# A retention layer and a Mish layer on one core: the first tiles' keys for the states turned back by TensorE, the decay moved into the keys, and three steps moved

## The chip, the core and the metric

The kernel runs on one core of one Trainium2 chip. The metric is the device time of one execution in microseconds. Fewer is better. The profile beside it is of one execution, recorded by the hardware profiler.

## What is computed

Attention without a softmax, with a decay that depends on the distance (retention), for 8 batches, 8 heads, 576 positions and heads of 64; its output, with the heads side by side, is x with 4608 rows of 512, and goes through two products (512 to 2048 and back) with a Mish between.

```python
scores = scale * np.matmul(q, k.transpose(0, 1, 3, 2))
gamma = 1.0 - 2.0 ** (-5.0 - np.arange(H, dtype=np.float32))
Dmat = np.where(rel >= 0, gamma[:, None, None] ** rel[None, :, :], 0.0)   # rel = pos[:, None] - pos[None, :]
ret = scores * Dmat[None, :, :, :]
attn = np.matmul(ret, v)                      # x: attn as (B * S, H * D)
h = x @ w_in
g = h * np.tanh(np.log1p(np.exp(h)))          # Mish
out = g @ w_out
```

## The kernel before

**Chunks and tiles.** The 576 positions of a batch are cut into chunks of 128 (and one of 64, two batches of which share a chunk). There are 36 chunks. Four chunks make a tile of 512 rows, so there are nine tiles; chunks 0 to 7 are the first 128 positions of the eight batches and make tiles 0 and 1. A chunk's output is the product of its own scores (masked) with v, and of q with a state, the sum of kᵀv over all positions ahead of it, with the decay multiplied into k or v. For each tile `g1` (L553) makes 16 blocks of Mish(x w_in), four products of 128x512 each, and `g2` (L569) or `g2_first` (L590) the product with w_out, 16 for each row block. These 128x512 products all go through `product` (L525), which can split one into two halves of 256 columns: `halved[0]` says how many of the next ones.

**The first two tiles** have a way of their own. `load_first_qk` (L102) loads q and k of four batches, cast to bf16 on the way; q of batches 0 and 1 comes as float32 by two loads of SyncE (L121) and is cast by VectorE (L639). `f_transpose` (L185) turns q and k, so that the head dimension lies on the partitions, `f_scores` (L208) makes the scores and multiplies them by the decay, `f_v` (L228) casts v, and `f_out` (L236) multiplies and copies the result to x of its tile (`xts`). In tile 0 each batch is copied by itself (L253), in tile 1 two batches at a time (L255). `keep_warm` (L167) issues products of zeros that nobody reads, which fill TensorE's waits at the start.

**The states of the first chunk.** When chunk 1 of a batch is handled, `states` (L383) also needs kᵀv of the batch's chunk 0. For that, `load_k0` (L263) loads k of the first 128 positions a second time, not turned, by GpSimd's queue, `cast_k0` (L267) casts it to bf16, and `f_state` (L257) multiplies v by the decay (`gv`). Loads, casts and products are spread over the whole kernel: a load each at L681, L712, L742, L785 and four at L815; casts at L729, L731 and by the table `cast_at` (L778).

**The other chunks** go two at a time through `visit` (L498), in this order on TensorE: part of the next pair's state products, this pair's outputs, the next pair's scores, the rest. `outputs_copy` (L485) then copies the two banks to `xts`, one by ScalarE and one by VectorE (L490), and `step_m` (L351) multiplies the next pair's scores by the mask. Ahead of that, each chunk needs `load` (q, k and v by GpSimd's queue), `step_p` (VectorE scales q and k, two instructions, L304), `step_v` (decay into v; GpSimd from chunk 20 on, L311) and `step_t` (turns q and k: by TensorE up to chunk 15, by a DMA transpose of SyncE from chunk 16 on, L333). `hold` (L492) makes GpSimd wait for such a transpose, and the loads behind it with it. `more_loads` can tie a load to a product of TensorE (`newest`), and `step_t` a transpose.

**The order is written out by hand.** Every engine takes its instructions in the order of the program. Tiles 0 and 1 are written as a list of calls and the table `steps` (L695): steps of tile 1 between the blocks of tile 0's second product. Then come 24 units (L726), and then a loop over the tiles from 2 on (L776) in which n is the pair of chunks visited and w a step of eight; the visit is at w = 6. There, of the chunks n+4 and n+5, one is scaled at w = 4 and the other at w = 7 (transpose behind each) as long as n+4 is at most `NPE` = 18; later both are scaled at w = 4 and 5 and turned at w = 6.

PSUM: scores, transposes and tile 1's outputs share the slots "sc" (two, of two banks each), blocks of `g1` the slots "hp" (two), row blocks "ops" (one), and the states "st" (one).

Of the kernel before, what the change touches and what calls it, by code (L numbers as in the profile page):

```python
# [16 lines left out]
def kernel(  # L17
# [100 lines left out]
        nc.gpsimd.dma_start(out=pair, in_=v[ds(b, 2), :, 0:P, :].rearrange("b h p d -> p (b h) d"))  # L118

    for b in range(2):  # L120
        nc.sync.dma_start(out=q0[:, b, :], in_=q[b, :, 0:P, :].rearrange("h (g r) d -> g h (r d)", r=8))  # L121
    for b in range(2):
        load_first_qk(0, 1, b)

# [103 lines left out]
    def f_v(t, b, copy):  # L228
        vb = first.tile([P, H, D], BF16, name="vb", bufs=4)
        copies = copy if isinstance(copy, tuple) else (copy,)  # L230
        n = H // len(copies)
        for j, copy in enumerate(copies):
            copy(vb[:, ds(n * j, n), :], v0[4 * t + b][:, ds(n * j, n), :])
        fst[t]["vb"][b] = vb

    def f_out(t, b, copy):  # L236
        if b == 0:
            xts[t] = xp.tile([P, KC, NCH * P], BF16, name="xT")
        vb = fst[t]["vb"][b]
        if t == 0:  # L240
            pool, name = ((ps_h, "hp"), (ps_h, "hp"), (ps_st, "st"), (ps_o, "ops"))[b]
            ot = pool.tile([P, NP, P], F32, name=name)
        else:
            if b % 2 == 0:
                fst[1]["out"] = ps_sc.tile([P, 2, NP, P], F32, name="sc")
            ot = fst[1]["out"][:, b % 2]
        for p in range(NP):
            for e in range(2):
                nc.tensor.matmul(ot[ds(64 * e, 64), p, :], lhsT=vb[:, 2 * p + e, :],
                                 rhs=fst[t]["sm", b][:, 2 * p + e, :],  # L250
                                 start=(p == 0), stop=True, skip_group_check=True)
        if t == 0:
            copy(xts[t][:, :, ts(b, P)], ot)  # L253
        elif b % 2:
            copy(xts[1].rearrange("p h (b i) -> p b h i", i=P)[:, ds(b - 1, 2)], fst[1]["out"])  # L255

    def f_state(t, b, engine=nc.gpsimd):  # L257

        n = 4 * t + b
        v0s[n] = first.tile([P, H, D], BF16, name="v0s", bufs=B)  # L260
        engine.tensor_tensor(v0s[n], v0[n], gv[:, 0, :].unsqueeze(2).to_broadcast([P, H, D]), op=OP.mult)

    def load_k0(b):  # L263
        k0r[b] = first.tile([P, H, D], F32, name="k0r", bufs=2)
        nc.gpsimd.dma_start(out=k0r[b], in_=k[b, :, 0:P, :].rearrange("h p d -> p h d"))

    def cast_k0(b, copy=nc.scalar.copy):  # L267
        k0[b] = first.tile([P, H, D], BF16, name="k0", bufs=3)
        copy(k0[b], k0r[b])

# [380 lines left out]
    keep_warm(1)  # L653
    f_out(0, 0, act)
    f_out(0, 1, act)
    keep_warm(5, ps_st, "st")
    load_w_in(1536, 512)
    f_v(0, 3, (dve, dve))
    f_v(0, 2, (act, pool))
# [17 lines left out]
                                base=0, pattern=[[1, 64]], channel_multiplier=-1)  # L677
    for b in range(4):
        load(N0 + b)
        if b == 0:  # L680
            load_k0(0)  # L681
    nc.vector.tensor_scalar(gq, gq, 1.0 / math.sqrt(D), None, op0=OP.mult)
    for b in range(4):
        f_state(0, b, nc.vector)


    for f in range(2):
        g1(0, f, 2, begun[f])
    g1_pair(2)
    for f in range(4, nF):  # L690
        halved[0] = 2 if f > 6 else 1
        g1(0, f)
    for i in range(2):
        f_mix(0, i)
    steps = {0: "T0", 3: "S0 C1", 9: "T1", 11: "S1", 12: "V0 V1 V2 V3", 14: "O0 O1", 15: "O2 O3"}  # L695
    for i in range(nF):
        for step in steps.get(i, "").split():
            n = int(step[1])
            if step[0] == "T":
                for j in range(2):  # L700
                    f_transpose(1, n, j, [(ps_sc, "sc", (dve, act)[j])])
            elif step[0] == "S":
                f_scores(1, n)
            elif step[0] == "V":
                f_v(1, n, dve if n == 3 else act)
            elif step[0] == "C":
                for j in range(2):
                    f_mix(n, j)
            else:
                f_out(1, n, (dve, act)[n // 2])  # L710
        g2_first(i // 4, i % 4)
    load_k0(1)  # L712

    queued = [4 * NCH]

# [9 lines left out]
    ts_ = {3: 0, 7: 1, 12: 2, 14: 3, 19: 4, 21: 5}  # L725
    for u in range(24):  # L726
        j, w = divmod(u, 4)
        if u == 5:
            cast_k0(0)  # L729
        elif u == 14:  # L730
            cast_k0(1, dve)  # L731
        halved[0] = 2 if 0 < u < 6 else 0
        if u in ps:
            att(N0 + ps[u], "P")
        if u == 11:
            step_m(N0)
        if u in vs:
            att(N0 + vs[u], "V")
        if w == 0 and j > 0:
            if j < 5:  # L740
                if j == 4:
                    load_k0(2)  # L742
                load(N0 + j + 3)
            else:
                load(N0 + j + 3)
                queued[0] += 1
        if u == 10:
            units, early = states(N0)
            seen = written(units[0]())
            step_s(N0)  # L750
            units[1]()
            units[2](seen)
            run(sums)
        elif u == 16:
            att(N0 + 4, "P")
        elif u == 17:
            visit(N0, ((ps_o, "ops"), (ps_h, "hp")), (act, act))
            run(sums)
        elif u == 22:
            visit(N0 + 2, ((ps_h, "hp"), (ps_h, "hp")), (act, dve))  # L760
        if u == 20:
            stores(act)
        if u in (13, 20):
            run(casts, dve if u == 13 else act)
        if u in ts_:
            att(N0 + ts_[u], "T")
        stores()
        if u < nF:
            g1(1, u, 2 if u == 0 else 1)
            flush()  # L770
        else:
            g2(1, u - nF)


    cast_at = {12: 2, 16: 3, 20: 4, 22: 5, 26: 6, 30: 7}
    for t in range(2, nT + 1):  # L776
        for i in range(nF):
            n, w = NCH * (t + 1) + i // 8 * 2, i % 8  # L778
            if w == 2 and n in cast_at:
                cast_k0(cast_at[n])  # L780
            if w == 2:
                run(casts, act)
                halved[0] = {14: 16, 20: 29}.get(n, 0)
            if w == 6 and n + 4 == NPE:
                load_k0(3)  # L785
            if w == 6 and n < n_chunks:
                visit(n, ((ps_h, "hp"), (ps_h, "hp")), (act, dve), lambda: g2(t - 1, i))
            if w == 0:
                stores(act if n == N0 + 4 else dve)
                run(sums)  # L790
            if w == 7 and n + 2 == NPE:
                stores()
            if w in (0, 1) and n + 2 < NT:
                att(n + 2 + w, "P")
            if w in ((3, 4) if n + 2 < NPE else (0, 1)):
                att(n + 2 + (w in (1, 4)), "V")
            if w in ((4, 7) if n + 4 <= NPE else (4, 5)) and n + 4 >= NT:
                stores()
                att(n + 4 + (w != 4), "P")
            if w == 7 and NT <= n + 4 <= NPE:  # L800
                step_t(n + 5, newest[0])
            if w == 5 and 16 <= n < 24:
                f_state(1, n // 2 - 8, nc.vector)


            if w in (1, 3) and n + 2 == NT:
                more_loads(n + 5 + w // 3, newest[0])
            if w == 1 and n + 2 == NPE:
                more_loads(n + 5, newest[0])
            if w == 1 and NPE < n + 2 < n_chunks:  # L810
                hold(n + 2)
            if w == 1 and n + 2 >= NPE:
                more_loads(n + 7)
                if t in (3, 4):
                    load_k0(2 * t - 2 + i // 8)  # L815
            if w in (4, 5) and n + 2 < NT:
                att(n - 2 + w, "T")
            stores()


            if t == 2:
                if w == 6:
                    g2(1, 8 + i // 2)
                g1(t, i)
                if w == 6:
                    step_t(n + 4, newest[0])
                if i % 2 and w != 7:
                    g2(1, 8 + i // 2)
            elif t == nT:
                if i < 12:  # L830
                    g2(t - 1, i)
            elif w == 6:

                last = n < n_chunks <= n + 2
                g2(t - 1, i + last)
                g1(t, i)
                if NPE < n + 4 < n_chunks:
                    for x in (4, 5):
                        step_t(n + x, newest[0])
            elif w == 7 and n < n_chunks <= n + 2:  # L840
                g1(t, i)
            elif i % 4 == 0:
                g1(t, i)
                g1(t, i + 1)
                g2(t - 1, i)
            else:
                if i % 4 != 1:
                    g1(t, i)
                g2(t - 1, i)
# [32 lines left out]
```

## Time and profile before

| | |
|---|---|
| three runs | 298.27, 298.43, 302.54 us; median 298.43 |
| the profiled execution | 298.47 us, its span 296.8 us |
| TensorE busy | 287.3 us (97%), 3442 instructions |
| weight loads busy | 157.1 us (53%) |
| VectorE, ScalarE, GpSimd busy | 138.3, 133.1, 128.0 us |
| DMA | 47.97 MB, mean 162 GB/s |
| GpSimd's DMA queue | 32.25 MB, 51.4% of the engines' time |
| instruction DMA | 27 packets and 0.44 MB on one queue, 8 and 0.07 MB on another |

How to read it: the span runs from the first instruction to the last. The chain of waits follows the last instruction back, at each step to what released it. A row of the timeline gives start, duration, engine, line, operation, what is written and read, how many, and in brackets the idle time ahead of it with what ended that. PE is TensorE's products, PEld its weight loads, DVE VectorE, ACT ScalarE, POOL GpSimd, SP SyncE. A TensorE product of 128x512 stands in the rows with some 0.38 us, as its passage through the array is counted; the next one starts 0.216 us behind it.

### The profile page before, as it was taken

Reading aid. Unit: us, or ns where it says so; the run is one execution under the profiler, and the core shown is the slowest. Engines: PE = TensorE matmul, PEld = TensorE weight load, DVE = VectorE, ACT = ScalarE, POOL = GpSimd, SP = SyncE. Lnnn points to the kernel's source line nnn. Section 1 sums busy time; section 2 is a strip of 40 time slices with the busy share of each in tenths; the row PEclk is TensorE's granted clock in tenths of the full one; section 3 lists DMA queues with packets and bytes.
Section 4 is the critical chain, followed back from the end, with each engine's and each line's share of the span. In section 5 each row is a group of like instructions: output and inputs, shape, how many; then the busy total and the mean of one; then the engine's idle time right before and its main releaser. Section 6 shows DMA issues by size and latency. Waiting matters only on the chain.

```text
span 296.8 us, 7900 instructions
## 1 busy us (share of the span) xinstructions
PE 287.3 (97%) x3442; PEld 157.1 (53%) x3480; DVE 138.3 (47%) x251; ACT 133.1 (45%) x219; POOL 128.0 (43%) x167
## 2 busy tenths in 40 slices
PE   8899999999999999999999999999999999999996
PEld 3466887555456544457645454545454544444443
DVE  5841646697955828453546453535354222010011
ACT  4866126776665444444363435343434433433200
POOL 8845756666818195557384727283020000000000
PEclk9999999999999999999999999999999999999999
DMA  7999999999989999998979868686314110110131
GB/s 159 223 201 205 205 239 216 339 228 211 258 200 187 178 228 239 176 246 204 201 192 203 207 159 209 145 204 145 83 48 95 38 38 37 37 35 35 53 91 71
DMA packets 42275, 47.97 MB, mean 162 GB/s; under 512 B 23936, under 2 KB 31104, under 8 KB 42240
## 3 DMA queue, kind: packets, MB, share of 16 engines
q0 software_dynamic: 15440, 32.25, 51.4%
q1 hardware_dynamic: 26656, 15.01, 21.3%
q8 instruction: 27, 0.44, 0.7%
q10 hardware_dynamic: 144, 0.20, 0.2%
q14 instruction: 8, 0.07, 0.1%
HBM read 38.80 MB, written 9.44 MB: 163 GB/s over the span
## 4 chain that ended last, share of the span: by engine, by line
PE 78%; DMA 14%; POOL 4%; issue 2%; DVE 2%; DVEq 0%; POOLq 0%
PE hp L527 37%; PE ops L527 29%; DMA vpair<-in_v_dram 4%; DMA w_out_t<-in_moe_w_out_dram 4%; DMA w_in_t<-in_moe_w_in_dram 3%; DMA qkraw<-in_k_dram 2%; PE hp L532 2%; PE ops L532 2%; PE sc L347 1%; PE sc L402 1%; PE hp L478 1%; PE hp L608 1%; PE hp L461 1%; POOL gT L107 1%; PE sc L325 1%
## 5 line engine op out<-in xcount | busy, mean ns | idle before, releaser
L527 PE MATMUL hp<-xT,w_in_t 128*128 128x512 bf16 (+1 forms) x507 | 126.5, 376 | 1.2 <-DVE xT L490 0.4
L564 ACT ACTIVATE gT<-hp 128x512 bf16<-128x512 f32 x142 | 84.8, 598 | 91.1 <-PE hp L527 84.6
L527 PE MATMUL ops<-w_out_t,gT 128*128 128x512 bf16 x411 | 101.9, 379 | 2.0 <-issue 1.9
L527 PEld LDWEIGHTS <-w_in_t 128*128 128x128 bf16 x528 | 51.4, 98 | 53.9 <-issue 0.9
L527 PEld LDWEIGHTS <-gT 128*128 128x128 bf16 x478 | 45.5, 98 | 52.6 <-issue 0.6
L616 DVE COPY res<-ops 128x512 f32<-128x512 f32 x28 | 19.3, 690 | 89.5 <-PE ops L527 89.5
L304 DVE TENSOR_TENSOR qks<-qkraw,gqk 128x512 bf16<-128x512 f32 x56 | 35.3, 683 | 7.3 <-DMA qkraw<-in_k_dram 7.3
L282 POOL DMA_DIRECT2D qkraw<-in_q_dram x24 | 21.5, 896 | 14.5 <-PE hp L527 7.0
L311 POOL TENSOR_TENSOR vs<-vraw,gv 128x512 bf16<-128x512 f32 x16 | 16.4, 1044 | 17.2 <-PE hp L461 17.1
L282 POOL DMA_DIRECT2D vraw<-in_v_dram x24 | 21.4, 893 | 3.1 <-DMA vpair<-in_v_dram 1.5
L282 POOL DMA_DIRECT2D qkraw<-in_k_dram x24 | 21.2, 885 | 2.4 <-DMA qkraw<-in_q_dram 0.9
L490 DVE CAST xT<-hp 128x512 bf16<-128x512 f32 x13 | 9.0, 691 | 27.1 <-PE hp L478 27.1
L490 ACT CAST xT<-hp 128x512 bf16<-128x512 f32 x14 | 8.2, 586 | 28.5 <-PE hp L478 28.5
L532 PEld LDWEIGHTS <-gT 128*128 128x128 bf16 x164 | 15.7, 98 | 3.2
L438 DVE TENSOR_TENSOR total<-sc,total 128x256 f32<-128x256 f32 x40 | 16.9, 421 | 1.0
L496 POOL COPY held<-qkT 128x1 bf16<-128x1 bf16 x8 | 1.5, 189 | 36.6 <-DMA qkT<-qks 36.6
L353 DVE TENSOR_TENSOR sm<-sc,mask 128x1024 bf16<-128x1024 f32 x14 | 17.0, 1215 | 0.3 <-PE sc L347 0.3
L532 PE MATMUL hp<-xT,w_in_t 128*128 128x256 bf16 x102 | 15.7, 272 | 0.0
L532 PEld LDWEIGHTS <-w_in_t 128*128 128x128 bf16 x104 | 10.2, 98 | 6.8 <-issue 0.4
L441 ACT CAST ssb<-total 128x768 bf16<-128x768 f32 (+3 forms) x13 | 11.7, 896 | 1.7 <-DVE total L438 1.6
L527 PE MATMUL hp<-w_out_t,gT 128*128 128x512 bf16 x49 | 12.0, 379 | 0.2 <-issue 0.2
L532 PE MATMUL ops<-w_out_t,gT 128*128 128x256 bf16 x80 | 10.4, 273 | 0.1
(126 smaller groups left out, 251.7 us busy)
## 6 DMA issues: line engine op xcount, KB each, us to landing
out_dram<-res SPq DMA_DIRECT2D x31, 256.0 KB, 3.0
qkraw<-in_q_dram POOLq DMA_DIRECT2D x24, 256.0 KB, 6.4
qkraw<-in_k_dram POOLq DMA_DIRECT2D x24, 256.0 KB, 6.7
vraw<-in_v_dram POOLq DMA_DIRECT2D x24, 256.0 KB, 6.9
w_out_t<-in_moe_w_out_dram POOLq DMA_DIRECT2D x4, 512.0 KB, 11.8
k0r<-in_k_dram POOLq DMA_DIRECT2D x8, 256.0 KB, 7.7
gT<-in_k_dram POOLq DMA_DIRECT2D x8, 128.0 KB, 6.3
gT<-in_v_dram POOLq DMA_DIRECT2D x2, 512.0 KB, 7.4
```

The lines of the kernel that those rows point to most:

```text
L107: nc.gpsimd.dma_start(out=fst[t][name][:, b, :], in_=(q, k)[i][4 * t + b, :, 0:P, :].rearrange("h (g r) d -> g h (r d)", r=8))
L282: ins = nc.gpsimd.dma_start(out=t, in_=src[b, :, ds(P * c, P), :].rearrange("h p d -> p h d"))
L304: nc.vector.tensor_tensor(slots[:, :, y], heads[:, :, y], factors[:, :, y].unsqueeze(3).to_broadcast([P, NP, 2, D]), op=OP.mult)
L311: engine.tensor_tensor(vs, live[n]["v"], gv[:, c, :].unsqueeze(2).to_broadcast([P, H, D]), op=OP.mult)
L353: nc.vector.tensor_tensor(sm.rearrange("p e x n i -> p (e x n) i"), live[n]["sc"].rearrange("p e x n i -> p (e x n) i"), mask.unsqueeze(1) ...
L438: nc.vector.tensor_tensor(new[:, k], st[:, j, x], total[b], op=OP.add)
L441: casts.append(lambda copy: copy(lows[:, 0:k], new[:, 0:k]))
L490: copy(xts[t][:, :, ds(P * s, 2 * P)].rearrange("p h (x j i) -> p j h x i", x=2, j=2)[:, j], both[j])
L527: newest[0] = nc.tensor.matmul(to, lhsT=w, rhs=x, start=first, stop=last)
L532: nc.tensor.matmul(to[:, ts(j, n)], lhsT=w, rhs=x[:, ts(j, n)], start=False, stop=False, skip_group_check=True)
L564: done = nc.scalar.activation(gts[t][:, f, :], hp, AX.Mish)
L616: copy(ot, ops)
```

## The change

Seven edits in one:

- q of batch 1 is loaded by ScalarE's queue in place of SyncE's.
- For batches 0 to 3, k of the first tile isn't loaded a second time. `turn_back` turns the turned k of `f_transpose` back by 16 TensorE transposes into one slot "sc", and `keep_back` copies it to SBUF, two copies by VectorE. Three of the five warm products at L656 go. Four loads and four casts of k go.
- For batches 4 to 7 the decay is multiplied into k by its cast, which is now a product of VectorE, and v's cast of `f_v` is used as it is. Four `f_state` products of VectorE and four ScalarE casts go.
- In tile 1, `f_out` of all four batches stands in one place (i = 15), with a copy for each batch, by VectorE and ScalarE in turn.
- At n = 16, chunk 21 is scaled and turned at w = 7, behind the visit, as it was for the pairs before.
- Fewer products are halved: in tile 0 from f = 4 on none up to 6 and then one for each f (before: one, then two); in tile 1 the units 1 to 4 (before 1 to 5).
- The slots follow: v0s 4 in place of 8, and 2 for the turned back k.

```diff
     for b in range(2):
-        nc.sync.dma_start(out=q0[:, b, :], in_=...)
+        (nc.sync, nc.scalar)[b].dma_start(out=q0[:, b, :], in_=...)
...
         fst[t]["vb"][b] = vb
+        if t == 1:
+            v0s[4 + b] = vb
...
-        if t == 0:
-            copy(xts[t][:, :, ts(b, P)], ot)
-        elif b % 2:
-            copy(xts[1].rearrange("p h (b i) -> p b h i", i=P)[:, ds(b - 1, 2)], fst[1]["out"])
+        copy(xts[t][:, :, ts(b, P)], ot)
-    def f_state(t, b, engine=nc.gpsimd):
-        n = 4 * t + b
-        v0s[n] = first.tile([P, H, D], BF16, name="v0s", bufs=B)
-        engine.tensor_tensor(v0s[n], v0[n], gv[:, 0, :].unsqueeze(2).to_broadcast([P, H, D]), op=OP.mult)
+    def f_state(b):
+        v0s[b] = first.tile([P, H, D], BF16, name="v0s", bufs=4)
+        nc.vector.tensor_tensor(v0s[b], v0[b], gv[:, 0, :].unsqueeze(2).to_broadcast([P, H, D]), op=OP.mult)
+    def turn_back(g):
+        if g == 0:
+            fst["back"] = ps_sc.tile([P, 4 * NP, P], BF16, name="sc").rearrange("p (g h) t -> p g h t", g=2)
+        for h in range(H):
+            nc.tensor.transpose(fst["back"][:, g, h, :], fst[0]["kb", g][:, h, :], ident)
+    def keep_back(g, copy):
+        both = first.tile([P, 2, H, D], BF16, name="back", bufs=2)
+        for x in range(2):
+            k0[2 * g + x] = both[:, x]
+        copy(both.rearrange("p x h d -> p h x d"), fst["back"][:, g].rearrange("p h (x d) -> p h x d", x=2))
...
-    def cast_k0(b, copy=nc.scalar.copy):
+    def cast_k0(b):
         k0[b] = first.tile([P, H, D], BF16, name="k0", bufs=3)
-        copy(k0[b], k0r[b])
+        nc.vector.tensor_tensor(k0[b], k0r[b], gv[:, 0, :].unsqueeze(2).to_broadcast([P, H, D]), op=OP.mult)
...
     f_out(0, 1, act)
-    keep_warm(5, ps_st, "st")
+    for g in range(2):
+        turn_back(g)
+    keep_warm(2, ps_st, "st")
...
         load(N0 + b)
-        if b == 0:
-            load_k0(0)
     for b in range(4):
-        f_state(0, b, nc.vector)
+        f_state(b)
+    for g in range(2):
+        keep_back(g, dve)
...
-        halved[0] = 2 if f > 6 else 1
+        halved[0] = int(f > 6)
         g1(0, f)
...
-    steps = {..., 12: "V0 V1 V2 V3", 14: "O0 O1", 15: "O2 O3"}
+    steps = {..., 12: "V0 V1 V2 V3", 15: "O0 O1 O2 O3"}
...
-                f_out(1, n, (dve, act)[n // 2])
+                f_out(1, n, (dve, act)[n % 2])
...
-    load_k0(1)
...
-        if u == 5:
-            cast_k0(0)
-        elif u == 14:
-            cast_k0(1, dve)
-        halved[0] = 2 if 0 < u < 6 else 0
+        halved[0] = 2 if 0 < u < 5 else 0
...
-                if j == 4:
-                    load_k0(2)
...
-    cast_at = {12: 2, 16: 3, 20: 4, 22: 5, 26: 6, 30: 7}
+    cast_at = {20: 4, 22: 5, 26: 6, 30: 7}
...
-            if w == 6 and n + 4 == NPE:
-                load_k0(3)
...
-            if w in ((4, 7) if n + 4 <= NPE else (4, 5)) and n + 4 >= NT:
+            if w in ((4, 7) if n + 4 <= NPE + 2 else (4, 5)) and n + 4 >= NT:
                 stores()
                 att(n + 4 + (w != 4), "P")
-            if w == 7 and NT <= n + 4 <= NPE:
+            if w == 7 and NT <= n + 4 <= NPE + 2:
                 step_t(n + 5, newest[0])
-            if w == 5 and 16 <= n < 24:
-                f_state(1, n // 2 - 8, nc.vector)
...
                 if NPE < n + 4 < n_chunks:
-                    for x in (4, 5):
+                    for x in ((4, 5) if n + 4 > NPE + 2 else (4,)):
                         step_t(n + x, newest[0])
```

More of the change, by code (lines that the diff above doesn't have):

```diff
@@ L120 @@
     for b in range(2):
-        nc.sync.dma_start(out=q0[:, b, :], in_=q[b, :, 0:P, :].rearrange("h (g r) d -> g h (r d)", r=8))
+        (nc.sync, nc.scalar)[b].dma_start(out=q0[:, b, :], in_=q[b, :, 0:P, :].rearrange("h (g r) d -> g h (r d)", r=8))
     for b in range(2):
@@ L694 @@
         f_mix(0, i)
-    steps = {0: "T0", 3: "S0 C1", 9: "T1", 11: "S1", 12: "V0 V1 V2 V3", 14: "O0 O1", 15: "O2 O3"}
+    steps = {0: "T0", 3: "S0 C1", 9: "T1", 11: "S1", 12: "V0 V1 V2 V3", 15: "O0 O1 O2 O3"}
     for i in range(nF):
```

## Prediction

> **What bounds the kernel now.** I read the first part of the page, then the waits by engine, then the chain of waits, then the timeline at the four places that the diff touches.
>
> The page's busy line, and from the list of who waited for whom the rows of TensorE (us in total, times, longest):
>
> ```profile
> PE 287.3 (97%) x3442; PEld 157.1 (53%) x3480; DVE 138.3 (47%) x251; ACT 133.1 (45%) x219; POOL 128.0 (43%) x167
> ```
>
> ```profile
> PE ops L527 <- issue: 1.9, 12, 0.2
> PE ops L170 <- DVE pos L135: 1.3, 1, 1.3
> PE sc L219 <- DVE sm L223: 0.5, 1, 0.5
> PE hp L527 <- DVE xT L490: 0.4, 1, 0.4
> PE hp L249 <- POOL vb L233: 0.3, 1, 0.3
> ```
>
> TensorE is busy 97% of 296.8 us. Of its 9.5 idle us 3.2 lie in the last 17 us (the tail) and about 2.5 in the first 16; the rest is spread in pieces of 0.05 to 0.4. VectorE, ScalarE and GpSimd are busy less than half the time, so work taken off them is worth time only where TensorE waits for them. From 16 us on, one such wait is left: 0.4 us for an xT of L490. So the change can win little, and I look for where it can lose.
>
> That wait in the chain (start, us, what):
>
> ```profile
> 112.23 0.68 DVE qks L304
> 112.92 0.60 DVE v0s L261
> 113.52 0.61 DVE xT L490
> 114.13 0.04 issue
> 114.17 1.02 PE hp L527 x4
> ```
>
> and TensorE in the timeline around it:
>
> ```profile
> 112.76 1.03 PE L527 MATMUL hp<-xT,w_in_t 128*128 128x512 bf16 x4
> ...
> 114.17 1.02 PE L527 MATMUL hp<-xT,w_in_t 128*128 128x512 bf16 x4 [0.38 <-DVE xT L490]
> ```
>
> Four products take 0.86 us (the chain's "L527 x4" elsewhere), so the next group could start at 112.76 + 0.86 = 113.62. It starts at 114.17: 0.55 us lost. Its bank of PSUM is freed by VectorE's copy to xT, which stood in VectorE's queue behind the scaling of chunk 21 (qks, waiting for a DMA until 111.6) and one decay product (v0s).
>
> The second place is the end of the first tile's second product, where the second tile's x comes in:
>
> ```profile
> 45.48 0.43 DVE vb L233
> 45.91 0.60 DVE res L616
> 46.51 1.14 DVE xT L255
> 47.65 0.04 issue
> 47.69 1.25 PE hp L527 x9
> ```
>
> TensorE shows no gap ahead of 47.69, yet VectorE releases it only at 47.65: the two arrive together, with nothing to spare. The chain ahead of this is one DMA, the last pair of v, landing at 45.36.
>
> The third is the start (timeline):
>
> ```profile
> 1.26 5.30 PE L170 MATMUL ops<-zeros 128*128 128x512 bf16 x12 [1.26 <-DVE pos L135]
> ...
> 13.16 1.25 PE L170 MATMUL st<-zeros 128*128 128x512 bf16 x5
> 14.13 0.70 DVE L233 CAST vb<-gT 128x256 bf16<-128x256 f32 x2 [0.20 <-DMA gT<-in_v_dram]
> ...
> 14.48 0.14 PEld L249 LDWEIGHTS <-vb 128*64 128x64 bf16 x4 [0.56 <-DVE vb L233]
> ...
> 14.88 0.36 PEld L249 LDWEIGHTS <-vb 128*64 128x64 bf16 x12 [0.26 <-DVE vb L233]
> ```
>
> Batch 3's products wait for v's cast in two halves; its second half runs from 14.88 whatever TensorE does before.
>
> **The change, part by part.** The sum goes against the profiled execution: 298.47 us, its span of 296.8 and 1.67 around it. The median of the three runs is 298.43, so the two agree.
>
> *q of batch 1 from ScalarE's queue.* It starts some 0.6 us earlier (SyncE's two issues took 1.33 us). Its reader, the second cast at L639, runs straight behind the first with no idle time on VectorE, so the data was there: worth 0. On ScalarE an issue of 0.57 to 0.70 us (SyncE's rows) stands ahead of a table load of 1.28 us; ScalarE idled 2.78 us before 4.87, which covers it; uncovered, 0.7. Later transfers may land a little earlier or later: ±0.2.
>
> *Keys turned back.* TensorE loses 3 warm products of 0.216 and gains 16 transposes. Eight of that form start 0.45 us apart as a group (29.28 and 29.73), so 0.90. Net +0.25 busy. On the path: 13.16 + 0.90 + 2×0.216 + 0.1 for changing over = 14.59, against 14.48 for the first half of batch 3 and 14.88 for its second; the first half needs 0.14, so 0.15 us is still free: 0. Uncovered it costs 0.25. It needs a PSUM slot of the scores (second round, first half), whose last reader is the sixth of eight sm products of 0.61 from 9.06, done at 12.7: in time. If the tracker held it to the eighth, at 13.93, batch 3 would start some 0.6 late; this is an end of the range. On VectorE the two copies cost 1.23 each (L205's 128x1024 bf16 copy from PSUM), from 18.41, where the four v0s end, to 20.9; VectorE idles until 27.04: 0. Their PSUM slot is next wanted at 29.7.
>
> *Loads and casts of k that go.* Four loads of 256 KB: four issues of 0.88 on GpSimd and 1 MB of traffic. No TensorE wait behind 16 us ends in a load except through the scaling of chunk 21, so 0. Chunk 9 to 11's loads move up one place in GpSimd's queue (it waits there for the eighth transfer back: 42.49 and 45.65 each for a vpair); VectorE's scaling waits for those (2.52 us at 52.56), TensorE doesn't. Seven casts of 0.61 leave ScalarE and one of 0.58 VectorE; no TensorE wait is theirs.
>
> *Decay in k for batches 4 to 7.* Four v0s of 0.68 leave VectorE, four casts of 0.68 come, at the third step of visits 20, 22, 26 and 30. There VectorE idles 4 to 5 us before the next stored row (5.45 ahead of 138.08), so 0; and k was loaded two visits or more before. The cover gone, 0.68 each on VectorE, 2.7 in all.
>
> *The one step moved past a visit.* Scaling of chunk 21 (two VectorE products, 1.29 in all) and its DMA transpose (one on SyncE) go behind visit 16's xT and mask product. VectorE then has nothing between 109.05 and the end of the visit's products; xT runs 112.0 to 112.6, beside ScalarE's at 111.92, a second ahead of need: −0.55. Next on VectorE: mask product 1.21 to 113.8, scaling to 115.1, then the stored row, which waited for TensorE at 116.09 with 0.84 idle: not late. On SyncE chunk 20's transpose still goes first at 113.86, holding the queue 1.24, so chunk 21's starts at 115.1 as before; the stores behind it (120.78) and GpSimd's held copy and loads behind that (121.86) stay. Chunk 21's transpose is needed at 127.06; its landing takes 7.7: slack 4. The visits before 16 already have this order, and TensorE shows no wait on them. Bounds: 0 to −0.55.
>
> *O0 to O3 together, one copy each.* TensorE changes over once less each way: −0.2 (gaps of 0.09 and 0.11 beside each group). Then VectorE: vb to 45.83, two stored rows at 0.60 to 47.03, O0's copy to about 47.7, O2's to 48.31. ScalarE: vb to 46.06, a row, O1's to 47.1, O3's to 47.6. TensorE would be ready at 47.69 − 0.2 = 47.5 but gets O0 at 47.75; after 0.43 of half products it wants O2 at 48.18 and gets it at 48.36. Before, that second half began at 48.12. So +0.24. Lower end −0.2 (all copies in time), upper +0.4 (alone, a copy takes 0.69 and not 0.60). I take +0.2: the DMA that starts this may land a little earlier.
>
> *Fewer halved products.* 12 fewer in the first tile, 2 in the second. Two halved take 0.44 against 0.43: 14 × 0.005 = −0.05 (the page shows a pitch of 0.867 against 0.863, which gives −0.03). TensorE's stream changes by +32 − 6 − 24 − 4 = −2 instructions, so the small "issue" gaps (0.16 and 0.05 each) hardly move: ±0.2.
>
> Sum: 298.47 − 0.55 + 0.2 − 0.05 = 298.1 us.
>
> **The rivals.** *The copies are hidden* (0.20): the pair of v lands 0.3 us earlier, and TensorE keeps its saved 0.2. For it: 1.33 us of issue made shorter at a saturated start. Against: the chain of DMAs, not q, sets 45.36. 298.47 − 0.55 − 0.2 − 0.05 = 297.7.
>
> *The stall at 114 only changes its cause* (0.15): xT is still late, or the transpose of chunk 21, late itself, holds up visit 18. Then 298.47 + 0.24 − 0.05 = 298.7. Against: visits 12 and 14.
>
> *TensorE's slow phase comes back at the start* (0.04), the case on the slow side. The first 12 warm products took 0.43 us each, the later five 0.216: for some 5.2 us TensorE ran at half its rate (the page's granted clock shows 1.0 all the same). Three of the warm products go. If the slow phase returned for as long at 14.5, where TensorE is dense from 15.3 on, it would lose 5.2 / 2 = 2.6; the waits at 47.7 would then be covered: 298.47 − 0.55 − 0.2 − 0.05 + 2.6 = 300.3. It decides if what is left near 13 us no longer counts as work. Against it: 16 transposes in a row at 29.28 are followed by products at full pace (four in 0.87).
> The Trainium skill, page "TensorE: Matmul & The Clock Gate", section "Part 4: PE-mode transpose", says that transposes don't count as busy time for the clock; the row at 29.28 shows 0.9 us of them doing no harm, but there full products stand on both sides. By that page's window of about 3.4 us the loss would be an estimated 1.7 us and not 2.6, so 299.4.
>
> **How the numbers follow.** The forecast has 0.58, its own range 297.6 to 298.6 (bounds of the copies and of the issue gaps); the three rivals 0.20, 0.15 and 0.04; 0.03 is for what I have not seen. 298.1 is the likeliest. From 297.4 to 299.0 the first three cases lie inside with their bounds and the slow phase outside: 8 in 10, with what I leave for unseen waits. Two per cent is 6 us, about what a measurement of this kernel can tell from no change; no named case reaches it, so within it 0.96, and 0.02 on each side.
>
> **What would show it.** Right: no TensorE wait for L490 near 113; VectorE's xT there before its scaling; a new TensorE wait of 0.1 to 0.3 us near 47.7 to 48.3 for an xT of the second tile; 16 transposes at 13.2 in 0.9 us and batch 3's second half at about 14.9; the two 128x1024 copies inside VectorE's gap of 18 to 27. Wrong: products at 0.43 us behind 14.5; batch 3 starting behind 15; a wait for qkT at visit 18, or for a VectorE copy at visits 20 to 30.

## The result, and the profile after

The changed kernel takes 301.19 us (median of 22 runs, 299.61 to 303.49) beside 298.40 us for the one before (22 runs): ratio 1.0093, 95% interval 1.0073 to 1.0114. That is 2.8 us longer where 0.3 less was forecast, and outside the range of 297.4 to 299.0. The ratio leaves out runs in a slower state, which are more than 1.5% above the fastest of their kernel: four of the 22 before (302.49 to 303.94 us), none after. The profiled execution took 301.42 us with a span of 299.7.

The page of the kernel after, its busy line and the granted clock in 40 slices of 7.5 us:

```profile
PE 288.1 (96%) x3440; PEld 157.3 (52%) x3479; DVE 140.1 (47%) x253; ACT 129.9 (43%) x213; POOL 124.9 (42%) x163
...
PEclk9999997999999999999999999999999999999999
```

TensorE's busy time rose by 0.8 us and its span by 2.9, so it waits more. And in the seventh slice (45 to 52.5 us) its granted clock, the share of full speed that the chip lets it run at, is lower. The list of who waited for whom, after, rows of TensorE (us in total, times, longest; "issue" is time in which the engine waited for nothing that the profile shows):

```profile
PE sc L251 <- DVE xT L254: 2.4, 2, 1.6
PE ops L538 <- issue: 1.9, 12, 0.2
```

The wait for L490 (0.4, now line 501) is gone. A new row stands at the top: products of `f_out` (L251) that wait for a copy of `f_out` (L254), 1.6 and 0.8 us. The chain of waits after, from v's arrival to the first product of the second tile:

```profile
45.26 0.43 DVE vb L233
45.68 1.20 DVE res L627 x2
46.88 0.61 DVE xT L254
47.49 0.04 issue
47.53 0.65 PE sc L251 x16
48.18 0.02 issue
48.21 0.70 DVE xT L254
48.91 0.04 issue
48.95 0.64 PE sc L251 x8
49.59 1.40 PE st L543 x6
50.98 0.22 issue
51.20 1.82 PE hp L538 x9
```

TensorE in the timeline before, where the same products run sixteen at a time and wait for no copy:

```profile
44.69 0.64 PE L249 MATMUL sc<-sm,vb 128*64 128x128 bf16 x16
...
46.24 0.64 PE L249 MATMUL sc<-sm,vb 128*64 128x128 bf16 x16
46.81 0.83 PE L532 MATMUL st<-w_out_t,gT 128*128 128x256 bf16 x6
```

and after, the same stretch:

```profile
45.50 0.41 PE L251 MATMUL sc<-sm,vb 128*64 128x128 bf16 x8
47.53 0.64 PE L251 MATMUL sc<-sm,vb 128*64 128x128 bf16 x16 [1.61 <-DVE xT L254]
48.95 0.64 PE L251 MATMUL sc<-sm,vb 128*64 128x128 bf16 x8 [0.78 <-DVE xT L254]
49.52 1.46 PE L543 MATMUL st<-w_out_t,gT 128*128 128x256 bf16 x6
```

O0 to O3 are the `f_out` of the four batches of tile 1. Their products do not run as one block of 32. They run as 8 (O0), 16 (O1 and O2) and 8 (O3). O1 waits until O0 has been copied, and O3 until O2 has been. O0 and O1 share one PSUM slot of two banks, O2 and O3 the other. So the chain now alternates: product, copy, product, copy, product, and behind them the rest of row block 3, before the next tile. The next tile starts at 51.20, where it was 47.69.

The last of that stretch is slow too: the six half products at 49.59 take 1.40 us (in the timeline's rows 1.46, where before it was 0.83). The windows of 1 us, after (the length, then PE, PEld, DVE, ACT and POOL busy, then the granted clock, the DMA's share and GB/s):

```profile
48.00:49.00 1.00, 0.22 (x8) 0.08 (x5) 0.79 (x2) 0.57 (x1) 0.54 (x1) 0.97 1.04 217
49.00:50.00 1.00, 1.00 (x11) 0.70 (x11) 1.00 (x2) 0.37 (x1) 0.78 (x1) 0.50 1.02 213
...
52.00:53.00 1.00, 1.00 (x9) 0.71 (x7) 0.99 (x2) 0.06 (x2) 0.71 (x2) 0.82 1.04 350
```

TensorE's clock is halved from 48.95 to 52.36, for 3.41 us by the trace's record of the clock, and so it loses 3.41 / 2 = 1.7 us.

By its rows the difference adds up. The second tile starts 3.51 later, and the part of the half clock behind 51.20 adds 0.57 by 67 us. Then the gaps named "issue" lie otherwise between 67 and 78 (−0.33), a gap of 0.25 at 104 is gone, and the stall at 114 too (from one visit's g2 products to the next: 112.11 to 127.70 before, 115.60 to 130.65 after, 15.59 against 15.05, −0.54). Sum: 3.51 + 0.57 − 0.33 − 0.25 − 0.54 = 2.96, and the spans differ by 2.9.

The 22 runs fall in three groups by their mean granted clock: nine at 0.999 to 1.0 (median 299.77 us), nine at 0.993 or 0.994 (301.45) and four at 0.987 or 0.988 (303.1). The steps are 1.7 us each, one halved stretch. So in 13 of 22 runs the clock falls, in four of them, by the size, twice; those second stretches weren't seen in a trace.

### The profile page after: what moved, and what is told of

Same layout as the page of the kernel before. It is cut to its first block, busy times and chain, and to the rows that moved or that the text cites. A ratio compares the mean times of both kernels' runs of the same rounds, so it can differ in the third digit from the quotient of the medians.

```text
span 299.7 us, 7884 instructions
## 1 busy us (share of the span) xinstructions
PE 288.1 (96%) x3440; PEld 157.3 (52%) x3479; DVE 140.1 (47%) x253; ACT 129.9 (43%) x213; POOL 124.9 (42%) x163
## 4 chain that ended last, share of the span: by engine, by line
PE 82%; DMA 11%; POOL 3%; issue 2%; DVE 1%; POOLq 0%; DVEq 0%
PE hp L538 38%; PE ops L538 30%; DMA w_out_t<-in_moe_w_out_dram 4%; DMA vpair<-in_v_dram 4%; DMA w_in_t<-in_moe_w_in_dram 3%; PE ops L543 2%; PE hp L543 2%; PE sc L358 1%; PE sc L413 1%; PE hp L489 1%; PE hp L472 1%; PE hp L619 1%; POOL gT L107 1%; POOL w_in_t L87 1%; PE sc L336 1%
## 5 line engine op out<-in xcount | busy, mean ns | idle before, releaser
L538 PE MATMUL hp<-xT,w_in_t 128*128 128x512 bf16 (+1 forms) x520 | 129.4, 377 | 1.1 <-issue 0.2
L538 PEld LDWEIGHTS <-w_in_t 128*128 128x128 bf16 x542 | 53.0, 98 | 56.4 <-issue 0.6
L315 DVE TENSOR_TENSOR qks<-qkraw,gqk 128x512 bf16<-128x512 f32 x56 | 36.8, 710 | 1.8 <-DMA qkraw<-in_k_dram 1.8
L543 PE MATMUL hp<-xT,w_in_t 128*128 128x256 bf16 x74 | 12.0, 272 | 0.0
L543 PEld LDWEIGHTS <-w_in_t 128*128 128x128 bf16 x76 | 7.4, 98 | 5.4 <-issue 0.2
```

Of the source, the lines that this page charges most:

```text
L315: nc.vector.tensor_tensor(slots[:, :, y], heads[:, :, y], factors[:, :, y].unsqueeze(3).to_broadcast([P, NP, 2, D]), op=OP.mult)
L538: newest[0] = nc.tensor.matmul(to, lhsT=w, rhs=x, start=first, stop=last)
L543: nc.tensor.matmul(to[:, ts(j, n)], lhsT=w, rhs=x[:, ts(j, n)], start=False, stop=False, skip_group_check=True)
```

## The experiments

**The theory.** The O step (the `f_out` of the four batches in one place, with a copy for each) alone does it. One slot holds two batches, accesses to it are put in order by slot and not by bank, so a copy that stands between the two products stops TensorE. The idle time then costs the clock. Rivals: the other parts share in it; or the wait is for VectorE's queue; or the half clock comes from something else. Each ratio is against the kernel before, run beside the experiment (medians of 298.01 to 298.18 us).

**1. The O step as before, all else changed.**

```diff
-        copy(xts[t][:, :, ts(b, P)], ot)
+        if t == 0:
+            copy(xts[t][:, :, ts(b, P)], ot)
+        elif b % 2:
+            copy(xts[1].rearrange(...)[:, ds(b - 1, 2)], fst[1]["out"])
...
-    steps = {..., 15: "O0 O1 O2 O3"}          # copies (dve, act)[n % 2]
+    steps = {..., 14: "O0 O1", 15: "O2 O3"}   # copies (dve, act)[n // 2]
```

> The changed kernel with the outputs of tile 1 put back as before: O0 and O1 at i = 14, O2 and O3 at i = 15, one copy for each pair. Theory (TensorE's wait for the single copies, and the slow clock that follows it, are the whole loss): 298.4 - 0.55 - 0.05 = 297.9 us, no TensorE wait for L254 or L255 near 46 to 49, granted clock 1.0 in every run. Rival (the turned-back keys, the loads that went or the decay in the casts cost as well): 299 us or more.

Measured: 297.84 us (12 runs), ratio 0.998 (0.9959 to 1.0000), clock 0.999 or more in every run. The second tile's first product in its timeline:

```profile
47.90 1.25 PE L541 MATMUL hp<-xT,w_in_t 128*128 128x256 bf16 x9 [0.19 <-DVE xT L257]
```

It starts 3.3 us earlier than after the change. All of the loss is in the O step, and the other six edits together are worth −0.3 us by the medians (297.84 against 298.18) and −0.6 by the ratio, whose interval runs from −1.2 to 0.

**2. Only the O step, on the kernel before.**

> The kernel before with only the outputs of tile 1 changed (O0 to O3 together, one copy each). Theory: TensorE waits some 2.4 us near 46 to 49 for two VectorE copies; with a granted clock of 1.0 the time is about 298.4 + 1.8 = 300.2 us (the fastest runs of the changed kernel, 299.7, against the 297.9 that it should have without this step), and part of the runs have a clock near 0.994 or 0.988 and are 1.7 or 3.4 us longer. Rival (it is the sum of several parts): under 299.5 us with the clock at 1.0 throughout.

Measured: 300.46 us (7 runs), ratio 1.009 (1.0055 to 1.0126). Four runs at clock 1.0 lie at 299.8 to 300.5, two at 0.994 at 301.9 and 302.0, one at 0.987 at 303.0. The trace has the two waits (1.41 and 0.78 us) and the halved clock behind them. So the step needs nothing else of the change. At full clock it costs 299.77 − 297.84 = 1.9 us (after against experiment 1; the four runs here, median 300.06, are 1.9 behind the 298.18 of the kernel before as well), and each fall 1.7 more.

**3. Four products first, then four single copies** (on the changed kernel).

```diff
-        copy(xts[t][:, :, ts(b, P)], ot)
+        if t == 0:
+            copy(xts[t][:, :, ts(b, P)], ot)
+        return lambda: copy(xts[t][:, :, ts(b, P)], ot)
...
-                f_out(1, n, (dve, act)[n % 2])
+                moves.append(f_out(1, n, (dve, act)[n % 2]))
+                if n == 3:
+                    for move in moves:
+                        move()
```

> The changed kernel, but the products of O0 to O3 are issued first and the four single copies behind them, in the same order and on the same engines. Theory (a product into one bank of a slot waits for the copy out of its other bank, since the two are one tile): no such wait is left, so 298.1 us as the prediction had it, clock 1.0. Rival (single copies by themselves are too late for the next tile): a wait of L538 for xT near 47.7 and 299 us or more.

Measured: 298.42 us (12 runs), ratio 1.0002 (0.9987 to 1.0018), clock 0.999 or more. The 32 products run together now. But ScalarE's timeline shows what is left:

```profile
47.31 1.18 ACT L256 CAST xT<-sc 128x512 bf16<-128x512 f32 x2 [1.19 <-DVE xT L256]
```

and TensorE's:

```profile
47.95 1.41 PE L540 MATMUL hp<-xT,w_in_t 128*128 128x256 bf16 x9 [0.60 <-ACT xT L256]
```

ScalarE stands idle 1.19 us until VectorE has copied O0, before it copies O1 from the other bank of the slot. Two reads of one slot by two engines are put in order as well. That both copies write the same tile of x is not the reason: in experiment 4 the same two copies read two slots, and they overlap (ScalarE's O1 from 46.19 to 46.77, VectorE's O0 from 46.42 to 47.10). The waits hang on semaphores, by which the profile names a releaser, so the order is one that the built program holds. From VectorE's cast of the last v to the second tile's first product it takes 2.89 us here (45.06 to 47.95) and 2.21 in experiment 1 (45.69 to 47.90). That agrees with the 0.6 us by which the median is behind experiment 1.

**4. Other pairs to a slot.** O0 and O2 in one, O1 and O3 in the other; order, copies and engines as changed.

```diff
-            if b % 2 == 0:
-                fst[1]["out"] = ps_sc.tile([P, 2, NP, P], F32, name="sc")
-            ot = fst[1]["out"][:, b % 2]
+            if b < 2:
+                fst[1]["out", b] = ps_sc.tile([P, 2, NP, P], F32, name="sc")
+            ot = fst[1]["out", b % 2][:, b // 2]
```

> The changed kernel with O0 and O2 in one slot of PSUM and O1 and O3 in the other (before: O0 and O1, O2 and O3). Theory (the wait is for the slot and not for the bank): O1 doesn't wait, O2 waits for O0's copy by VectorE and O3 for O1's by ScalarE; one wait of some 1.5 us in place of two of 1.6 and 0.8, so 299.7 - 1.4 = 298.3 us at a clock of 1.0, and the clock falls in fewer runs than the changed kernel's two in three. Rival (the wait is for the bank, or for VectorE's queue whatever it writes): O1 waits as before and the time stays at 299.7 and more.

Measured: 299.05 us (12 runs), ratio 1.0028 (1.0012 to 1.0043), clock 0.999 or more in all. In its timeline the products run as 16 and 16:

```profile
47.16 0.64 PE L251 MATMUL sc<-sm,vb 128*64 128x128 bf16 x16 [1.00 <-DVE xT L254]
```

Now O1 doesn't wait, and O2 waits for the copy of O0. The wait went with the slot, though each batch still has a bank for itself and the order, the copies and the engines stayed the same: it is by slot. The time is 0.75 above what was expected. The expectation named a wait of 1.5 that stays, but took 1.4 off for it, which fits a wait of 1.0. The profiled run, with its wait of 1.00, took 298.53 and is the fastest of the twelve; the waits of the others weren't traced.

**5. The waits filled.** On the changed kernel, products of zeros added to an open sum, seven behind O0 and three behind O2.

```diff
                 f_out(1, n, (dve, act)[n % 2])
+                for _ in range((7, 0, 3, 0)[n]):
+                    nc.tensor.matmul(outs[0, 3], lhsT=zeros[:, 0:P], rhs=zeros, start=False, stop=False, skip_group_check=True)
```

> The changed kernel with 7 products of zeros behind O0 and 3 behind O2, added onto a bank that is being summed anyway, so that TensorE works while it waits for the copies. Theory (the slow clock comes from the two idle stretches): the waits' length stays, the clock doesn't fall: 299.7 us in every run, granted clock 0.999 or more. Rival (the clock falls for another reason, or the loss is the waits alone): the runs spread over 299.7, 301.4 and 303.1 us as they do without the filling, or the time rises above 300.5.

Measured: 301.17 us (6 runs), ratio 1.0091 (1.0072 to 1.0111), clock 0.999 or more in all. The clock stays up, as the theory says, but the time is above its bound. The timeline has a new gap, far away:

```profile
105.65 1.25 PE L538 MATMUL ops<-w_out_t,gT 128*128 128x512 bf16 x5 [0.90 <-issue]
```

TensorE's stream is 20 instructions longer in this kernel, so I gave them back.

**6. The waits filled, stream of the same length.** Experiment 5 with ten fewer halved products.

```diff
-        halved[0] = int(f > 6)
+        halved[0] = 0
...
-        halved[0] = 2 if 0 < u < 5 else 0
+        halved[0] = (0, 2, 2, 2, 1)[u] if u < 5 else 0
```

> As e4_wait_filled (10 products of zeros in TensorE's waits), but with 10 fewer products halved, so that TensorE's stream is as long as that of the changed kernel (6960 instructions; e4 had 6980). Theory (e4 kept the clock up, and its extra 1.4 us over the changed kernel's undisturbed runs is the stretch of 0.90 us at 105.65 in which TensorE waited for nothing but its own stream, moved there by 20 instructions): 299.7 to 299.9 us, clock 1.0 in every run, and no issue gap above 0.3 us near 105. Rival (the products of zeros cost this themselves): 301.2 us again.

Measured: 299.93 us (5 runs), ratio 1.0064 (1.0047 to 1.008), clock 0.999 or more. The gap at 105 is gone (visit to visit 14.44 us, as elsewhere, against 15.51). What is left is the cost of the waits in time without the clock's, as in the nine runs of the changed kernel at full clock (299.77).

**7 and 8. One wait filled, the other left.** First the zeros behind O2 only (three; `halved` at f > 9), then behind O0 only (seven; f > 13).

> The changed kernel with 3 products of zeros behind O2 alone (TensorE's stream kept at 6960 instructions by 3 fewer halved): the first wait of 1.6 us stays, the second is filled. Theory (the clock falls when a stretch of about the length of the slow one, 3.4 us, holds too little work: the two waits together leave 2.4 idle of 3.5): the clock stays at 1.0 in nearly all runs and the time is 299.7 to 299.9 us. Rival (1.6 us of idle time are enough): 0.994 or less in about half of the runs, and those are 1.7 us longer.

> The changed kernel with 7 products of zeros behind O0 alone (7 fewer halved): the second wait of 0.8 us stays. Theory as for e10, and its rival too: clock 1.0 in every run, 299.7 to 299.9 us. A fall here would mean that neither wait's length decides.

Measured: with the first wait left 300.75 us (6 runs), ratio 1.0083 (1.0055 to 1.0111), two of them at a clock of 0.994 (301.31 and 301.78). With the second left 300.30 us (5 runs), ratio 1.0069 (1.0045 to 1.0093), none below 0.999; that is some 0.4 more than was expected, which stays unexplained. The trace of the second has no record of the clock, but its six half products behind the waits run at full pace (0.83 us from 49.50). The profiled run of the first has this ahead of a fall at 48.79:

```profile
48.01 0.64 PE L251 MATMUL sc<-sm,vb 128*64 128x128 bf16 x16 [2.03 <-DVE xT L254]
```

I had expected both waits to be needed. That fell: one wait of 2.03 us was followed by a fall. Waits of 1.0 (experiment 4), 0.72 (6) and 0.78 (8) were not, in 12, 5 and 5 runs. Two of six is few. The waits are those of the profiled runs. The kernel before also has runs at 0.994 or less, 5 of the 76 beside these experiments, not traced.

**9. Only the move of chunk 21, on the kernel before.**

```diff
-            if w in ((4, 7) if n + 4 <= NPE else (4, 5)) and n + 4 >= NT:
+            if w in ((4, 7) if n + 4 <= NPE + 2 else (4, 5)) and n + 4 >= NT:
```

(and the two lines on `step_t` as in the change)

> The kernel before with only chunk 21's scaling and transpose moved behind visit 16. Theory (that step of the prediction): TensorE's wait for L490 at 114 goes, nothing takes its place: 298.2 - 0.55 = 297.65 us. Rival (another wait of the same visit, or the decay product that is still there, takes its place): 298.0 to 298.4 us and a TensorE wait for L490 or for the transposed chunk.

Measured: 298.48 us (12 runs), ratio 1.0016 (0.999 to 1.0042): no gain in the time. The nine runs at full clock have a median of 298.13; three are at a clock of 0.994 (301.72 to 303.18 us), without the waits of the O step, and weren't traced. VectorE's timeline has what was forecast:

```profile
112.03 0.69 DVE L490 CAST xT<-hp 128x512 bf16<-128x512 f32 x1 [2.22 <-PE hp L478]
112.64 1.21 DVE L353 TENSOR_TENSOR sm<-sc,mask 128x1024 bf16<-128x1024 f32 x1
113.77 2.79 DVE L304 TENSOR_TENSOR qks<-qkraw,gqk 128x512 bf16<-128x512 f32 x2
```

xT comes ahead of the scaling, and visit to visit takes 15.05 us in place of 15.59. In this execution the second tile began 0.44 later than before (48.13), behind the last v, which hides the gain. The move works where it is made; that it is worth 0.5 in the time isn't shown.

**10. Only the keys turned back, on the kernel before** (`turn_back`, `keep_back`, four loads and casts out, as in the diff; decay, O step and chunk 21 as before).

> The kernel before with only the turned-back keys: 16 transposes in place of 3 warm products, two VectorE copies, four loads and casts of k less, and 12 fewer halved products; v0s in four slots, for room. Theory (that step of the prediction): hidden at the start, so the same as before within 0.2 us, 298.0 to 298.3, with batch 3's second half at 14.9. Rival (a saving through the 1 MB less of loads, or a cost at the start): 0.4 us or more to either side.

Measured: 297.70 us (12 runs), ratio 0.9977 (0.9956 to 0.9997): a small gain. The stall at 114 is gone here as well, though chunk 21 was not moved (visit to visit 15.05). VectorE's timeline:

```profile
110.64 1.29 DVE L317 TENSOR_TENSOR qks<-qkraw,gqk 128x512 bf16<-128x512 f32 x2 [1.83 <-DMA qkraw<-in_k_dram]
111.85 0.69 DVE L261 TENSOR_TENSOR v0s<-vpair,gv 128x512 bf16<-128x512 f32 x1
112.45 0.68 DVE L503 CAST xT<-hp 128x512 bf16<-128x512 f32 x1
```

and before:

```profile
111.62 1.29 DVE L304 TENSOR_TENSOR qks<-qkraw,gqk 128x512 bf16<-128x512 f32 x2 [2.58 <-DMA qkraw<-in_k_dram]
```

The scaling of chunk 21 starts at 110.64, where it was 111.62: its k is issued from 104.2 on in both and lands about a microsecond sooner. The load of batch 3's keys, which stood ahead of it in the queue at 95.0, is gone; that this is the reason is argued from the order of the queue and not shown.

**11. Copies ahead of a row block's.** On the changed kernel: four products together, the two pair copies right behind them, and the copy of row block 2 of the first tile after these.

```diff
-        if part == 3:
+        if part == 3 and s != 2:
...
+                f_out(1, n, (dve, act)[n // 2])
+                if n == 3:
+                    for b, copy, both in pairs:
+                        copy(xts[1].rearrange(...)[:, ds(b - 1, 2)], both)
+                    store(0, 2, outs[0, 2], nc.vector.tensor_copy)
```

> The changed kernel with the four products together ahead of any copy, one copy for each pair as before the change, and VectorE's copy of row block 2 behind its copy to xT. Theory (the next tile waits for VectorE's queue: cast, two row blocks, copy): without the second row block the copy to xT ends 0.6 us earlier, TensorE starts the next tile at some 47.4, not at 47.9 as in e1: 297.84 - 0.45 = 297.4 us. Rival (the last pair of v sets it, whatever VectorE's order): 297.8 us.

Measured: 297.81 us (11 runs), ratio 0.999 (0.9977 to 1.0003), no better than experiment 1. Its second tile starts at 47.56, still behind the copy:

```profile
47.56 1.25 PE L543 MATMUL hp<-xT,w_in_t 128*128 128x256 bf16 x9 [0.18 <-DVE xT L731]
```

The gain was not there to be had: VectorE has one row block ahead of this copy in both kernels. From its cast of the last v to the second tile's first product it takes 2.22 us here (45.34 to 47.56), 2.21 in experiment 1 and 2.21 before (45.48 to 47.69), so v's arrival moves this place. What a row block less would bring is not tested. The run does show that the four products together cost nothing when the copies stand behind them: the loss is in the copies between.

**12. Experiment 1 with q of batch 1 left to SyncE.**

> e1_pairs_again with both loads of q by SyncE's queue as before. Theory (that step is worth nothing): 297.84 us as e1, within 0.3. Rival (q of batch 1 from ScalarE's queue shifts the loads of k or v at the start): 0.4 us or more to either side, and a TensorE wait for k or v at the start that differs.

Measured: 297.77 us (12 runs), ratio 0.9988 (0.9974 to 1.0003), against 297.84 and 0.998 with ScalarE's queue: the move is worth nothing that these runs can tell.

## Why the prediction was wrong, step by step

- **"O0 to O3 together, one copy each": +0.2, bounds −0.2 to +0.4.** This is the step that failed. I counted the copies by themselves, and that was good: O0's copy ended at 47.49 (forecast 47.75, v being 0.2 earlier), one copy takes 0.61 to 0.70. What I left out is that O1's product waits for O0's copy, as the one writes and the other reads the same slot. "TensorE would be ready at 47.69 − 0.2 = 47.5" supposed all 32 products done by then; eight were. The lines to see it were in front of me: `f_out` takes one slot for two batches, and the copy moved in between their products. Measured: 1.9 us at full clock (experiments 1 and 2) where +0.2 stood, and 1.7 more for each fall of the clock.
- **The clock.** I had the slow phase as a rival with 0.04, 2.6 us, at the start. The mechanism was the one that came, the place was not. It came behind the new waits at 46 to 49, as 3.41 us at half rate, a loss of 1.7 each time. Experiments 2, 5 and 6 tie it to these waits: the O step alone brings it, zeros in the waits keep it away. They are not the only thing that brings it: experiment 9 has 3 such runs of 12 without them, the kernel before 5 of 76. The Trainium skill, page "TensorE: Matmul & The Clock Gate", section "Part 1: The HAM clock gate (the "warmup" mystery)", gives a free-running window of 3413 ns and a drop to half rate after an idle window. The length agrees with the trace (3.413 us, and the time at full clock ahead of it, 44.373 us, is 13 of these). That the whole window has to be idle does not: the one that ended at the fall, 45.54 to 48.95, holds 1.61 + 0.78 = 2.4 us of wait and 1.0 of products, and in experiment 7 it holds 2.03. The measurement decides. The 13 traces with a record of the clock narrow it down, cut into stretches of 3.413 us from the moment the clock came up. In the middle of the kernel the three stretches ahead of a fall have 2.03, 2.12 and 2.40 us without TensorE's products, all others 1.04 or less. At the end, where the products run out, the clock falls behind a stretch with 2.15 to 3.0 us without them (six traces) and does not behind one with 0.33 to 1.33 (seven). So the limit lies between 1.33 and 2.03 us; where, is open.
- **Keys turned back: 0 at the start.** Right. TensorE's rows after:

```profile
13.23 1.07 PE L266 MATMUL sc<-ident,qkT 128*128 128x128 bf16 x16
...
14.99 0.39 PE L251 MATMUL st<-sm,vb 128*64 128x128 bf16 x8
```

  Sixteen transposes in 0.9 us, batch 3's second half at 14.99 (before 15.02), and no slow phase behind them. The two copies took 1.28 us together, not 1.23 each. In VectorE's gap this costs nothing either way.
- **Loads and casts that go: 0.** Off by a little. I had named the way ("except through the scaling of chunk 21") and then counted the gain to the move alone. In experiment 10, with the loads gone and chunk 21 not moved, the stall is gone as well.
- **Chunk 21: −0.55.** Size right in the traces (−0.54 after, −0.54 in experiment 9), but not a second gain next to the keys': either edit ends the same stall. All parts but the O step give −0.3 by the medians and −0.6 by the ratio (experiment 1); −0.6 stood in the sum, and the runs can't tell the two apart.
- **q by ScalarE, decay in the casts, fewer halves: 0, 0, −0.05.** q: nothing, by experiment 12. The others weren't run alone; they lie within what experiment 1 gives for all six, and no TensorE wait in the trace after names them.
- **The range** held what I had thought of for the copies. It missed because the bounds of one step were worked out for the instruction's duration, not for a new order between engines.

## What to carry to other kernels

Before a copy is moved between two products, see which tile each of them writes: in this kernel two that shared a tile ran one behind the other with the copy between them, though each had its own bank, and two engines that read one tile took turns. A wait on the engine that bounds the kernel costs its length, and on TensorE possibly 3.4 us at half rate behind it, which lose 1.7; a few products of zeros in a wait that can't be removed kept the clock up here, and cost nothing more once the stream was kept as long as it was. Of two edits that end the same stall, count the gain once.

## What the runs showed of the hardware that was not expected

- The clock's rows lie on a grid of 3.413 us: in three kernels (after, experiments 2 and 7) it fell 44.373 us after it had come up, for 3.413 us, and every other stretch at full clock is a whole number of these too (249.173, 290.133 and 293.546 us are 73, 85 and 86). The clock came up between 4.1 and 7.1 us into the span, so the grid lies otherwise in each run. That would explain why the same waits bring a fall in some runs only, and times in steps of 1.7 us; the runs without a trace can't show it.
- Twenty more TensorE instructions brought a gap of 0.90 us at 105, some 56 us behind them, and ten fewer halved products took it away (experiments 5 and 6). The cause, the loading of the instruction stream, is argued from the name of the gap ("issue") and from the count, and not shown.
- VectorE's scaling of one chunk took 2.8 us in place of 1.29 when GpSimd's products of v ran beside it (experiment 9, the row at 113.77; GpSimd's two took 2.49 from 113.53, in place of 2.05 before). The Trainium skill, page "SBUF — State Buffer", section "🔬 SBUF: two separate sides", says that VectorE and GpSimd share a pair of ports that one of them locks for a whole instruction; the rows agree: each of VectorE's two ends some 0.55 us, about its own length, behind one of GpSimd's (114.57 and 115.12, 116.02 and 116.56). No TensorE wait follows it here.
